# Newton steps of six attention groups as one block-diagonal product, and an ordering estimate with other prices

## The chip, the cores and the metric

The kernel runs on one core of one Trainium2 chip. The metric is the device time of one execution in microseconds (us). Engines are named as the profile names them: PE is TensorE (matmul), PEld its weight loads, DVE VectorE, ACT ScalarE, POOL GpSimd, SP the queue that issues most transfers. Each engine runs its own instructions in the order in which the program wrote them.

## The reference

A Nystrom attention over 4 batches of 8 heads (576 tokens, head size 64, 32 landmarks) is followed by two feed-forward layers over the 2304 tokens. The 32x32 matrix of the landmarks is inverted by six Newton steps.

```python
A = sm(q, k_lm)
Bm = sm(q_lm, k_lm)
C = sm(q_lm, k)
Z = Bm.transpose(0, 1, 3, 2) / (norm1(Bm) * norminf(Bm) + 1e-06)
for _ in range(6):
    Z = 2 * Z - Z @ Bm @ Z
attn = A @ Z @ C @ v
...
h = x @ w_in            # layer 1: 2304 x 512 @ 512 x 2048
g = h * tanh(softplus(h))
x = g @ w_out
...
h = x @ w_in            # layer 2, with silu
g = h * (1.0 / (1.0 + np.exp(-h)))
out = g @ w_out
```

## The kernel before, in words

**Attention groups.** The 32 heads are worked in eight groups of four heads (`Group`, g = 0 to 7, two per batch), each head on 32 of the 128 partitions. A group makes transposes of k and q (tiles `Tk`, `Tq`), the landmark means (`lmT`), the scores (`Tk,lmT` and `Tq,lmT`), the softmax of C (`ec`, transposed to `ect` and multiplied with `vn`), the softmax of A (`at`, kept as `a_t`) and the matrix Bm (`eb`, `bn`). `newton` then runs the six steps. Its state `yu` has two parts per head: 32 columns that hold the iterated product and 64 columns that hold the right side, which is carried through the steps. A step is: PE makes `y` times `yu` of each head, DVE forms twice `yu` less the product. `each` writes the product of a step as four matmuls of 32x32 weights, one per head, each on its own 32 rows and 32 columns of the PE array (tiled matmuls below). At the end one matmul of `yu` with `bd`, the block-diagonal form of Bm scaled by `rc`, gives `ut`. `main` makes `bd` once, ahead of the Newton steps.

**Layers.** Layer 1 takes `ut` times the decoded weights (`wa`, the projection, tiled matmuls of 512 columns) to `wp`, then per unit six matmuls of 288 columns to `h` (`h<-at,wp`), Mish on ACT to `z`, a split of `z` in two halves `g` (ACT and POOL), and twelve matmuls of 288 columns to `y` (`y<-g,wo`). There are 128 units, 64 of them from the first half of the inner dimension, and the units of a batch need that batch's two groups done. Layer 2 (`h<-xg,wf`, `y<-wo,xg` and others) follows. The weights arrive as 64-bit words and are decoded by ACT, DVE and POOL (`wst` to `m`, `wa`, `wo`).

**What sets the order.** Nothing is ordered by hand. `Line` holds an estimate of when each engine will be free and when each tile will be written: every operation goes through `issue` (L196 to L226 in the profile), which adds `cost` to the estimated time and then writes the instruction. Chains (a group's `main`, `c_side`, `a_side`, a decode, a projection) are generators that are stepped when the estimate says that their input is ready (`step`, `run`), and the units of layer 1 are written between them. So a changed price changes where in each engine's order every later instruction stands, and which of two engines gets an operation that either can do. Where the estimate sees PE with too little work, before all groups are done, the main loop writes pairs of transposes of `ident` that nobody reads, in the PE order; they are called fillers below. Almost every instruction has line L226, since `issue` writes it.

**Tables of ACT.** Exp (for `eb`, `ec`, `at`), Mish and Silu come from tables that ACT has to load when it goes from one to another (`ACT_TABLE_LOAD`). The estimate before has no price for it.

Of the kernel before, what the change touches and what calls it, by code (L numbers as in the profile page):

```python
# [11 lines left out]
FP32 = mybir.dt.float32  # L12
# [47 lines left out]
def width(ap):  # L60
    return ap.size() // ap.shape[0]


class Line:
# [7 lines left out]
    WINDOW, ENOUGH = 4.096 / 1.2, 3060  # L72
    AGAIN = {"V": 0.12, "A": 0.12, "P": 0.1, "T": 0.0}
    FIXED = {"V": 0.07, "A": 0.1, "P": 0.05, "T": 0.0133}
    EACH = {"V": 1.04e-3, "A": 0.82e-3, "P": 2.29e-3, "T": 0.417e-3}

    def __init__(self, nc):
        self.nc = {"V": nc.vector, "A": nc.scalar, "P": nc.gpsimd, "T": nc.tensor}
        self.free = dict.fromkeys(["V", "A", "P", "T", "D", "W"], 0.0)
        self.now = 0.0  # L80
        self.free["D"] = 0.45
        self.end = 0.0
        self.last = set()
        self.past = collections.deque()
        self.held = {"V": collections.deque(), "P": collections.deque()}
        self.busy, self.seen = {}, {}
        self.chains = []
        self.small = False
        self.count = itertools.count()

    def cost(self, e, name, kw):
        src = kw.get("in_", kw.get("in0"))
        n = width(src if name == "tensor_reduce" else kw["out"])
        psum = src is not None and src.space == bass.MemoryType.PSUM
        more = 0.0
        if e == "T":
            tiled = kw["out"].shape[0] < 96 and "lhsT" in kw
            if tiled and (kw["out"].start_partition() or kw["lhsT"].start_partition()):
                return 0.027 * self.clock()
            n *= self.clock() * self.columns(kw)  # L100
        elif e == "A":
            more = -0.04 if psum else 0.0
            more += 0.14 if "accum_out" in kw else 0.09 if kw.get("func") == ACTF.Ln else 0.0
        elif e == "P" and name == "tensor_scalar":
            n *= 0.46
        elif e == "V" and name in ("copy", "tensor_copy", "tensor_scalar", "scaled"):
            if not psum:
                n *= 0.5
            elif n < 300:
                n += 50  # L110
            more = 0.06 if hasattr(kw.get("scalar1"), "space") else 0.0
        elif e == "V" and name == "reciprocal" and n > 1:
            more = 0.09
        elif e == "V" and name == "tensor_reduce" and n > 1000:
            more = 0.9
        return self.FIXED[e] + more + n * self.EACH[e]

    @staticmethod
    def span(ap):
# [71 lines left out]
    def issue(self, engines, name, kw, bias=0.0):  # L191
        def start(e):
            at = max(self.now, self.free[e], self.depend(e, name, kw))
            return self.alone(e, at, name, kw)

        e = min(engines, key=lambda e: start(e) + self.cost(e, name, kw) + (bias if e == "V" else 0.0))  # L196
        at = start(e)
        if e == "T":
            small = kw["out"].shape[0] < 96
            if self.small and not small:  # L200
                at = max(at, self.free["T"] + 0.055)
            self.small = small
        end = at + self.cost(e, name, kw)
        if e == "T":
            tick = int(at / self.WINDOW)
            rows = kw["lhsT" if "lhsT" in kw else "in_"].shape[0]
            part = rows * kw["out"].shape[0] / 16384 * self.columns(kw)
            self.past.append((at, width(kw["out"]) * part))
            self.busy[tick] = self.busy.get(tick, 0) + width(kw["out"]) * part
        if self.holds(e, name, kw):  # L210
            self.held[e].append((at, end))
            while len(self.held[e]) > 24:
                self.held[e].popleft()
        self.free[e] = end
        self.end = max(self.end, end)
        self.last.add(e)
        self.record(e, kw, end)
        if name == "copy" and e != "A":
            name = "tensor_copy"
        if name == "scaled":  # L220
            k = dict(out=kw["out"], in_=kw["in_"])
            if e == "A":
                name, kw = "activation", dict(k, func=ACTF.Copy, scale=kw["scalar1"])
            else:
                name, kw = "tensor_scalar", dict(out=kw["out"], in0=kw["in_"], scalar1=kw["scalar1"], scalar2=None, op0=ALU.mult)
        r = getattr(self.nc[e], name)(**kw)  # L226
        return r

    def transfer(self, engine, **kw):
        ap = kw["out"] if kw["out"].space == bass.MemoryType.SB else kw["in_"]  # L230
        start = max(self.now, self.free["D"], self.depend("D", "dma", kw))
        self.free["D"] = start + width(ap) * ap.shape[0] * 4 / 0.36e6
        end = self.free["D"] + 2.1
        self.end = max(self.end, end)
        self.last.add("D")
        self.record("D", kw, end)
        return engine.dma_start(**kw)  # L237
# [110 lines left out]
def kernel(  # L348
# [99 lines left out]
    def until(cond):  # L448
        while not cond():
            yield "W"  # L450
# [549 lines left out]
    class Group:  # L1000
# [98 lines left out]
        def main(self):  # L1099
# [37 lines left out]
            for h in range(HG):  # L1137
# [56 lines left out]
            Ring.give(py)  # L1194
            yield "V"

            bd = self.bd = s_p.tile([128, HG, LM], FP32, tag="bd", name="bd")
            V.scalar_tensor_tensor(
                out=bd,
                in0=bn.rearrange("p (o l) -> p o l", o=1).to_broadcast([128, HG, LM]),  # L1200
                scalar=rc,
                in1=mask,
                op0=ALU.mult,
                op1=ALU.mult,
            )
            marks.add((g, "y"))
            yield "T"
            yield from until(marked((g, "u")))
# [3 lines left out]
        def each(out, lhsT, rhs, **kw):  # L1212

            for h in range(HG):
                r = slice(32 * h, 32 * h + 32)
                T.matmul(out=out[r], lhsT=lhsT[r], rhs=rhs[r], start=True, stop=True)

        def newton(self):

            yu, g = self.yu, self.g  # L1220
            for it in range(6):
                lo = 0 if it < 5 else LM
                yield from until(self.banks.ready)
                pn = self.banks.take([128, LM + D], FP32)
                self.each(pn[0][:, lo:], yu[:, 0:LM], yu[:, lo:])
                yield "V"
                yn = s_p.tile([128, LM + D], FP32, tag="yu", name="yu", bufs=4)
                V.scalar_tensor_tensor(
                    out=yn[:, lo:], in0=yu[:, lo:], scalar=2.0, in1=pn[0][:, lo:], op0=ALU.mult, op1=ALU.subtract
                )  # L1230
                Ring.give(pn)
                yu = yn
                yield "T"
            yield from until(self.banks.ready)
            pu = self.banks.take([128, HG * LM], FP32)
            r = slice(64 * self.hg, 64 * self.hg + 64)
            T.matmul(
                out=pu[0][r], lhsT=yu[:, LM:], rhs=self.bd.rearrange("p h l -> p (h l)"), start=True, stop=True
            )
            yield "W"  # L1240
            VA.copy(out=ut_t[self.b][r].rearrange("p h l -> p (h l)"), in_=pu[0][r])
# [290 lines left out]
```

## Time and profile before

| what | value |
|---|---|
| time, median of 3 runs | 858.45 us (857.98 to 859.84) |
| span of the profiled execution, first to last instruction | 855.9 us |
| median less span, what lies around it | 2.55 us |
| PE busy | 824.3 us (96%) |
| DVE busy | 515.6 us (60%) |
| ACT busy | 450.6 us (53%) |
| POOL busy | 288.1 us (34%) |

The page gives the span of one execution. Attention lies in its first 223 us (beside layer 1 from about 50 us on), layer 1 ends at about 467 us, layer 2 at 849 us. An engine's busy time is the union of its instructions; on PE an instruction's row reaches past the start of the next one, so for PE the distance from start to start is what an instruction costs in a stream.

### The profile page before, as it was taken

How to read it: one execution, taken by the hardware profiler on the slowest of the kernel's cores; microseconds unless marked ns; L12 is line 12 of the kernel's file. 1: busy time of each engine (PE TensorE's matmuls, PEld its weight loads, DVE VectorE, ACT ScalarE, POOL GpSimd, SP SyncE). 2: the span in 40 equal slices, each digit the busy share in tenths (PEclk: the TensorE clock that was granted, in tenths of full speed). 3: DMA queues.
4: the chain of work that ended last, by engine and by line, in shares of the span. 5: the costliest groups of instructions: out<-in, count | busy, mean ns of one | idle time of the engine just before them, and what ended most of it. 6: DMA issues, size and time to landing. Idle time of an engine off the chain costs nothing.

```text
span 855.9 us, 15972 instructions
## 1 busy us (share of the span) xinstructions
PE 824.3 (96%) x6084; PEld 726.1 (85%) x6084; DVE 515.6 (60%) x1030; ACT 450.6 (53%) x997; POOL 288.1 (34%) x331
## 2 busy tenths in 40 slices
PE   7999989899999999999999999999999999999996
PEld 5877767676899989989999898898898898998885
DVE  4976644453586958414516999767555567555542
ACT  5574776667555565433425755544544454544432
POOL 4241524342355555624323434311223221232210
PEclk9999999999999999999999999999999999999999
DMA  9874225200345554241125422101400000200002
GB/s 246 237 224 154 59 55 139 57 29 2 106 148 176 157 197 155 80 129 56 57 79 156 152 99 87 37 1 38 111 1 1 0 1 8 67 1 2 0 1 75
DMA packets 42254, 72.36 MB, mean 85 GB/s; under 512 B 5056, under 2 KB 31680, under 8 KB 42176
## 3 DMA queue, kind: packets, MB, share of 16 engines
q1 hardware_dynamic: 41600, 70.54, 27.1%
q8 instruction: 48, 0.79, 0.4%
q10 hardware_dynamic: 576, 0.79, 0.3%
q14 instruction: 30, 0.25, 0.1%
HBM read 57.15 MB, written 14.16 MB: 83 GB/s over the span
## 4 chain that ended last, share of the span: by engine, by line
PE 86%; ACT 7%; DMA 3%; issue 1%; DVE 1%; SPq 1%; POOL 0%; ACTq 0%; POOLq 0%; DVEq 0%
PE y L226 47%; PE h L226 31%; PE t L226 8%; ACT L226 3%; ACT z L226 1%; DMA wst<-in_moe_w_in_dram 1%; SPq L237 1%; DMA kn<-in_k_dram 1%; ACT g L226 1%; ACT ec L226 1%; DMA wst<-in_moe_w_out_dram 1%; DMA wst<-ys 0%; ACT at L226 0%; DMA out_dram<-ysb 0%; ACT wp L226 0%
## 5 line engine op out<-in xcount | busy, mean ns | idle before, releaser
L226 PE MATMUL y<-g,wo 128*128 128x288 f32 x1536 | 235.0, 301 | 1.4 <-POOL g L226 1.4
L226 PEld LDWEIGHTS y<-g,wo 128*128 128x128 f32 x1536 | 209.8, 188 | 15.3 <-issue 9.8
L226 PE MATMUL y<-wo,xg 128*128 128x512 f32 x693 | 179.8, 394 | 0.0
L226 POOL TENSOR_TENSOR g<-z,g 128x288 fp32r<-128x288 f32 x128 | 114.5, 905 | 174.3 <-ACT g L226 150.5
L226 PEld LDWEIGHTS y<-wo,xg 128*128 128x128 f32 x693 | 128.4, 188 | 20.9
L226 DVE TENSOR_TENSOR z<-h,z 128x384 f32<-128x384 f32 x164 | 89.4, 554 | 70.9 <-PE h L226 68.8
L226 PE MATMUL h<-at,wp 128*128 128x288 f32 x768 | 121.0, 302 | 5.8 <-ACT z L226 5.7
L226 PEld LDWEIGHTS h<-at,wp 128*128 128x128 f32 x768 | 106.3, 188 | 19.1 <-ACT z L226 8.8
L226 ACT ACTIVATE z<-h 128x288 f32<-128x288 f32 x128 | 51.6, 413 | 73.9 <-PE h L226 71.5
L226 ACT ACTIVATE z<-z 128x384 f32<-128x384 f32 x94 | 49.2, 525 | 34.3 <-DVE z L226 34.0
L226 POOL TENSOR_TENSOR wo<-m,wo 128x512 fp32r<-128x512 f32 x32 | 46.5, 1454 | 54.7 <-ACT wo L226 47.7
L226 DVE SCALAR_TENSOR_TENSOR m<-wst,m 128x512 int32<-128x512 int32 x64 | 61.9, 968 | 1.1
L226 PE MATMUL h<-xg,wp 128*128 128x384 f32 x288 | 58.0, 336 | 1.5 <-DVE z L226 1.5
L226 PE MATMUL h<-xg,wf 128*128 128x384 f32 x288 | 57.9, 336 | 0.4 <-DVE z L226 0.4
L226 ACT CAST g<-z 128x288 fp32r<-128x288 f32 x123 | 51.8, 435 | 7.4 <-PE y L226 6.2
L226 PEld LDWEIGHTS h<-xg,wp 128*128 128x128 f32 x288 | 51.3, 188 | 5.0 <-DVE z L226 1.9
L226 PEld LDWEIGHTS h<-xg,wf 128*128 128x128 f32 x288 | 51.2, 188 | 3.9 <-DVE z L226 0.9
L226 DVE TENSOR_TENSOR xg<-z,xg 128x384 fp32r<-128x384 f32 x73 | 41.4, 570 | 20.9 <-ACT xg L226 20.6
L226 POOL TENSOR_TENSOR wf<-m,wf 128x256 fp32r<-128x256 f32 x20 | 16.2, 809 | 96.8 <-ACT wf L226 96.8
L226 PE MATMUL y<-wo,wp 128*128 128x512 f32 x171 | 44.9, 394 | 0.0
L226 ACT ACT_TABLE_LOAD x31 | 39.8, 1283 | 1.7 <-PEq L1516 0.7
L226 DVE TENSOR_TENSOR wp<-t,wp 128x512 fp32r<-128x512 f32 x32 | 20.6, 685 | 30.5 <-ACT wp L226 30.4
(229 smaller groups left out, 1179.8 us busy)
## 6 DMA issues: line engine op xcount, KB each, us to landing
wst<-in_moe_w_out_dram SPq DMA_DIRECT2D x32, 512.0 KB, 5.8
wst<-in_moe_w_in_dram SPq DMA_DIRECT2D x28, 512.0 KB, 5.4
kn<-in_k_dram SPq DMA_DIRECT2D x32, 144.0 KB, 5.3
vn<-in_v_dram SPq DMA_DIRECT2D x8, 576.0 KB, 6.1
yh<-ysb SPq DMA_DIRECT2D x32, 144.0 KB, 1.9
ysb<-yh SPq DMA_DIRECT2D x32, 144.0 KB, 2.9
ys<-ysb SPq DMA_DIRECT2D x32, 144.0 KB, 2.0
qn<-in_q_dram SPq DMA_DIRECT2D x28, 144.0 KB, 3.6
```

Source lines behind the costliest of these rows:

```text
L226: r = getattr(self.nc[e], name)(**kw)
L237: return engine.dma_start(**kw)
```

## The change

Two things are changed. For groups 2 to 7 a Newton step is one matmul of the whole array: `blocks` writes the current `y` of the four heads as a block-diagonal 128x128 matrix `bd` (one DVE operation with a mask), and one matmul with `bd` as weights takes the place of the four tiled ones. Groups 0 and 1 keep the tiled form. The block-diagonal form of Bm is now made after the last step, in the same tile. And the estimate in `Line` has other prices: ACT pays for a change of table, a tiled matmul has a price that depends on how many run at once, with a price for going to the tiled form and for going back, and rates of POOL, ACT, the fp32 transposes and the transfers are different.

```diff
-    EACH = {"V": 1.04e-3, "A": 0.82e-3, "P": 2.29e-3, "T": 0.417e-3}
+    EACH = {"V": 1.04e-3, "A": 0.82e-3, "P": 2.67e-3, "T": 0.417e-3}
+    TABLES = {ACTF.Exp: "exp", ACTF.Mish: "mish", ACTF.Silu: "silu"}
+    LOAD = 1.3
+    TO_TILES, FROM_TILES, WEIGHTS = 0.092, 0.273, 0.107
...
-            tiled = kw["out"].shape[0] < 96 and "lhsT" in kw
-            if tiled and (kw["out"].start_partition() or kw["lhsT"].start_partition()):
-                return 0.027 * self.clock()
+            if "lhsT" not in kw:
+                return 0.002 + n * 2 * self.clock() * self.EACH["T"]
+            if kw["out"].shape[0] < 96:
+                at_once = 128 // kw["out"].shape[0] * (2 if kw["lhsT"].shape[0] == 64 else 1)
+                if kw["lhsT"].shape[0] == 128:
+                    at_once = 1
+                first = 0.0 if self.small else max(0.0, self.WEIGHTS - n * 2 * self.EACH["T"])
+                return first + n * 4 * self.clock() * self.EACH["T"] / at_once
...
+            if self.table_of(name, kw) not in (None, self.table):
+                more += self.LOAD
...
-                at = max(at, self.free["T"] + 0.055)
+                at = max(at, self.free["T"] + self.FROM_TILES)
+            elif small and not self.small:
+                at = max(at, self.free["T"] + self.TO_TILES)
...
-        self.free["D"] = start + width(ap) * ap.shape[0] * 4 / 0.36e6
+        rate = 0.24e6 if ap.shape[0] < 64 else 0.3e6 if ap.shape[0] < 128 else 0.4e6
+        self.free["D"] = start + width(ap) * ap.shape[0] * 4 / rate
...
+        def blocks(self, y, by):
+
+            V.scalar_tensor_tensor(
+                out=self.bd,
+                in0=y.rearrange("p (o l) -> p o l", o=1).to_broadcast([128, HG, LM]),
+                scalar=by,
+                in1=mask,
+                op0=ALU.mult,
+                op1=ALU.mult,
+            )
...
             yu, g = self.yu, self.g
+            bd = self.bd.rearrange("p h l -> p (h l)")
+            whole = g > 1
             for it in range(6):
                 lo = 0 if it < 5 else LM
+                if whole:
+                    yield "V"
+                    self.blocks(yu[:, 0:LM], 1.0)
+                    yield "T"
                 yield from until(self.banks.ready)
                 pn = self.banks.take([128, LM + D], FP32)
-                self.each(pn[0][:, lo:], yu[:, 0:LM], yu[:, lo:])
+                if whole:
+                    T.matmul(out=pn[0][:, lo:], lhsT=bd, rhs=yu[:, lo:], start=True, stop=True)
+                else:
+                    self.each(pn[0][:, lo:], yu[:, 0:LM], yu[:, lo:])
...
+            yield "V"
+            self.blocks(self.bn, self.rc)
+            yield "T"
```

In the rows below, the counts are those of the program: a tiled or an fp32 matmul against weights is one row here and two instructions in the trace; a filler is one of both. All instructions of `issue` stand at L226 before and at L256 after.

PE, the last Newton steps of group 3, before. `yu` of 32x96 and 32x64 are Newton steps, `h<-at` and `y<-g,wo` units of layer 1, `lmT` the landmark scores of group 4:

```order
L226 MATMUL y<-g,wo 128x288 x6
L226 MATMUL t<-yu 32x96 x4
L226 MATMUL h<-at_637,wp 128x288 x2
L226 MATMUL t<-lmT 32x32 x4
L226 MATMUL h<-at_637,wp 128x288 x2
L226 MATMUL t<-yu 32x96 x4
L226 MATMUL h<-at_637,wp 128x288 x6
L226 MATMUL t<-yu 32x64 x4
```

The same steps of group 3 after:

```order
L256 MATMUL t<-yu,bd 128x96
L256 MATMUL y<-g,wo 128x288 x17
L256 MATMUL t<-yu,bd 128x96
L256 MATMUL y<-g,wo 128x288
L256 MATMUL t<-yu,bd 128x64
L256 MATMUL y<-g,wo 128x288 x13
L256 MATMUL t<-bd,yu 64x128
```

Each row of four tiled matmuls is one whole matmul now; between the last three steps stand 17 and 1 matmuls of layer 1, where 4 (with four small tiled ones) and 6 stood.

PE, the first two Newton steps of group 3, before (`ident,kn` and `ident,qn` are transposes of group 4):

```order
L226 MATMUL h<-at_637,wp 128x288 x2
L226 MATMUL t<-yu 32x96 x4
L226 MATMUL h<-at_637,wp 128x288 x2
L226 MATMUL t<-ident,kn 128x128 x3
L226 MATMUL h<-at_637,wp 128x288 x2
L226 MATMUL t<-yu 32x96 x4
L226 MATMUL y<-g,wo 128x288 x2
```

The second and the third step of group 3 after (`h<-ident` are fillers, `Tk,lmT` the scores of group 4):

```order
L256 MATMUL h<-ident 128x128 x4
L256 MATMUL t<-yu,bd 128x96
L256 MATMUL h<-ident 128x128 x2
L256 MATMUL t<-lmT 32x32 x4
L256 MATMUL h<-ident 128x128 x16
L256 MATMUL t<-Tk,lmT 32x288 x8
L256 MATMUL h<-ident 128x128 x2
L256 MATMUL y<-g,wo 128x288 x12
L256 MATMUL h<-at_671,wp 128x288 x6
L256 MATMUL h<-ident 128x128 x16
L256 MATMUL y<-g,wo 128x288 x2
L256 MATMUL t<-yu,bd 128x96
```

Where the order before has only matmuls of layer 1 between the steps, 40 fillers stand now.

PE, from the scores of group 5 to the next matmul that needs a bank of the ring `t`, before:

```order
L226 MATMUL t<-Tk,lmT 32x288 x8
L226 MATMUL h<-at_1334,wp 128x288 x4
L226 MATMUL y<-g,wo 128x288 x20
L226 MATMUL t<-Tq,lmT 32x288 x8
L226 MATMUL y<-g,wo 128x288 x4
```

The same place after:

```order
L256 MATMUL t<-Tk,lmT 32x288 x8
L256 MATMUL h<-at_1359,wp 128x288 x2
L256 MATMUL y<-g,wo 128x288 x24
L256 MATMUL h<-at_1359,wp 128x288 x10
L256 MATMUL t<-bt 32x32 x4
```

36 matmuls of layer 1 stand between the scores and the next user of a bank, where 24 stood.

Counted over the whole PE order: the Newton steps of groups 2 to 7 are 36 in both; the places where PE goes from other work to tiled matmuls fall from 94 to 61; the fillers rise from 208 to 292, all 84 of the difference ahead of layer 1's second half; the matmuls of the layers are the same in number. DVE has 36 more operations `bd<-yu,mask`, and ACT 29 table loads in place of 31.

## Rows read from the trace of the kernel before

**Rows 1.** The page: engine totals, and the chain that ended last, by engine.
```profile
PE 824.3 (96%) x6084; PEld 726.1 (85%) x6084; DVE 515.6 (60%) x1030; ACT 450.6 (53%) x997; POOL 288.1 (34%) x331
PE 86%; ACT 7%; DMA 3%; issue 1%; DVE 1%; SPq 1%; POOL 0%; ACTq 0%; POOLq 0%; DVEq 0%
```
**Rows 2.** Busy time by stretch: length; PE, PEld, DVE, ACT, POOL; clock, DMA share, GB/s.
```profile
0.00:47.00 47.00, 42.13 (x534) 33.73 (x534) 36.01 (x98) 24.61 (x62) 16.31 (x29) 1.00 0.90 242
47.00:83.20 36.20, 34.63 (x384) 26.56 (x384) 24.99 (x67) 23.75 (x50) 11.36 (x10) 1.00 0.59 193
83.20:223.40 140.20, 129.83 (x1447) 98.92 (x1448) 65.92 (x200) 97.44 (x200) 52.09 (x61) 1.00 0.21 57
...
sum 855.90, PE 824.32 PEld 726.11 DVE 515.64 ACT 450.64 POOL 288.11; mean PE 137.39 PEld 121.02 DVE 85.94 ACT 75.11 POOL 48.02
```
**Rows 3.** What PE waited for, us in total, times, longest.
```profile
PE t L226 <- ACT ec L226: 6.6, 6, 1.5
PE h L226 <- ACT z L226: 5.7, 8, 1.0
```
**Rows 4.** PE in order of time around two Newton steps: start, us, operation, count.
```profile
101.44 0.42 PE L226 MATMUL h<-at,wp 128*128 128x288 f32 x2
101.79 0.37 PE L226 MATMUL t<-yu 32*32 32x96 f32 x8
102.09 0.54 PE L226 MATMUL h<-at,wp 128*128 128x288 f32 x2
102.46 0.49 PE L226 MATMUL t<-ident,kn 128*128 128x128 f32 x3
102.71 0.51 PE L226 MATMUL h<-at,wp 128*128 128x288 f32 x2
103.15 0.37 PE L226 MATMUL t<-yu 32*32 32x96 f32 x8
103.45 0.54 PE L226 MATMUL y<-g,wo 128*128 128x288 f32 x2
```
**Rows 5.** PE in order of time: rates of whole matmuls, fillers, and of `bd,yu`.
```profile
42.22 2.17 PE L226 MATMUL t<-Tk,twice 128*128 128x128 f32 x18
...
48.01 1.75 PE L226 MATMUL y<-ident 128*128 128x128 f32 x14
...
83.54 0.43 PE L226 MATMUL t<-bd,yu 128*64 128x128 f32 x2
83.90 0.40 PE L226 MATMUL h<-at,wp 128*128 128x288 f32 x1
...
450.48 8.16 PE L226 MATMUL y<-g,wo 128*128 128x288 f32 x60
```
**Rows 6.** PE, then ACT, in order of time around the longest `ec` wait.
```profile
109.96 1.64 PE L226 MATMUL t<-Tk,lmT 64*32 64x288 f32 x16
111.53 2.89 PE L226 MATMUL y<-g,wo 128*128 128x288 f32 x20
115.93 0.43 PE L226 MATMUL t<-bd,yu 128*64 128x128 f32 x2 [1.51 <-ACT ec L226]
...
113.99 1.28 ACT L226 ACT_TABLE_LOAD   x1
115.28 0.50 ACT L226 ACTIVATE ec<-t,nmc 128x288 f32<-128x288 f32 x1
```
**Rows 7.** Groups of DVE and ACT over the whole span: busy us, mean ns, idle before.
```profile
L226 DVE SCALAR_TENSOR_TENSOR yu<-yu,t 128x96 f32<-128x96 f32 x35 | 8.8, 251 | 29.5 <-PE t L226 27.1 <-issue 2.3
L226 DVE SCALAR_TENSOR_TENSOR bd<-bn,rc,mask 128x128 f32<-128x128 f32 x8 | 4.6, 569 | 0.0
...
L226 ACT ACT_TABLE_LOAD x31 | 39.8, 1283 | 1.7 <-PEq L1516 0.7 <-PE h L226 0.4
```
**Rows 8.** PE in order of time: two Newton steps of group 7, one after the other.
```profile
212.44 0.37 PE L226 MATMUL t<-yu 32*32 32x96 f32 x8
...
213.47 0.37 PE L226 MATMUL t<-yu 32*32 32x96 f32 x8
```

More of the change, by code (lines that the diff above doesn't have):

```diff
@@ L88, in __init__ @@
         self.small = False
+        self.table = "exp"
         self.count = itertools.count()
@@ L96, in cost @@
         if e == "T":
[L97 to L99 removed]
+            if "lhsT" not in kw:
[6 more added lines that the diff above has]
+                return first + n * 4 * self.clock() * self.EACH["T"] / at_once
+            if n == 512:
+                more = 0.005
+            if self.columns(kw) == 4:
+                n = max(n, 64)
             n *= self.clock() * self.columns(kw)
@@ L102, in cost @@
             more = -0.04 if psum else 0.0
-            more += 0.14 if "accum_out" in kw else 0.09 if kw.get("func") == ACTF.Ln else 0.0
+            more += 0.1 if "accum_out" in kw else 0.0
+            if name == "scaled":
+                more += 0.1
+            if src is not None and not psum and abs(src.ap[-1][0]) == 2:
+                more += 0.045
+            if self.table_of(name, kw) not in (None, self.table):
+                more += self.LOAD
         elif e == "P" and name == "tensor_scalar":
             n *= 0.46
+        elif e == "P" and "in1" in kw and not kw["in1"].ap[-1][0]:
+            n *= 0.73
         elif e == "V" and name in ("copy", "tensor_copy", "tensor_scalar", "scaled"):
@@ L116, in cost, with table_of @@
         return self.FIXED[e] + more + n * self.EACH[e]
+    def table_of(self, name, kw):
+        return self.TABLES.get(kw.get("func")) if name == "activation" else None
     @staticmethod
@@ L198, in issue @@
         if e == "T":
-            small = kw["out"].shape[0] < 96
+            small = kw["out"].shape[0] < 96 and "lhsT" in kw
             if self.small and not small:
-                at = max(at, self.free["T"] + 0.055)
+                at = max(at, self.free["T"] + self.FROM_TILES)
+            elif small and not self.small:
+                at = max(at, self.free["T"] + self.TO_TILES)
+        end = at + self.cost(e, name, kw)
+        if e == "T":
             self.small = small
-        end = at + self.cost(e, name, kw)
+        elif e == "A":
+            self.table = self.table_of(name, kw) or self.table
         if e == "T":
@@ L1195, in main @@
             yield "V"
[L1197 to L1205, printed above, removed]
+            self.bd = s_p.tile([128, HG, LM], FP32, tag="bd", name="bd")
             marks.add((g, "y"))
@@ L1237, in newton @@
             T.matmul(
-                out=pu[0][r], lhsT=yu[:, LM:], rhs=self.bd.rearrange("p h l -> p (h l)"), start=True, stop=True
+                out=pu[0][r], lhsT=yu[:, LM:], rhs=bd, start=True, stop=True
             )
```

## The prediction

> **What bounds the kernel now.** I read the page's totals first: PE is busy 96% of the span and holds 86% of the chain that ended last; DVE, ACT and POOL have much free time [rows 1]. PE runs its instructions in order, so the span can be written as an account of PE alone: work of the layers and of attention, fillers, and waits. Whatever the change does to another engine counts only where it alters one of these three. The account by stretch [rows 2] shows where there are waits: 4.9 us of PE's first 47 us (47.00 less 42.13), 1.6 us up to 83.2, 10.4 us from there to the end of attention (140.20 less 129.83), and the rest of the 31.6 us (855.90 less 824.32) in the layers behind it and at the end, where the matmuls are the same in number before and after. The granted clock is 1.00, so 2.4 GHz, in each of these stretches, so the clock has no part in the sum. What PE waited for is ACT in nearly all cases: 6.6 us in 6 waits for `ec`, 5.7 us in 8 waits for `z` [rows 3].
>
> The cause of the longest of these waits can be read off. After the scores PE has 20 matmuls of layer 1 (111.53), and is then to write a bank which `ec` still reads. ACT had to load the table of Exp first, from 113.99 to 115.27; PE stood 1.51 us [rows 6]. There are 31 such loads of 1283 ns [rows 7], 39.8 us of ACT time for which the estimate that makes the order has no price.
>
> **The change part by part.**
>
> *Whole Newton steps.* What a visit to the tiled form costs PE is read from two visits: from 101.44 to 103.45 are 2.01 us [rows 4]. In them lie six matmuls of 288 columns, at 8.16/60 = 0.136 us, and three transposes at the rate of whole fp32 passes, 2.17/18 = 0.12 us [rows 5]: 0.82 + 0.36 = 1.18. The remaining 0.83 us are two visits, 0.42 us each, though the four matmuls themselves stand for 0.30 us (101.79 to 102.09); the rest is the way into the tiled form and out. Visits fall from 94 to 61, so 33 x 0.42 = 13.9 us go; three steps shared a visit with another tiled product and give only their own 0.30 each, 0.9 us. What takes their place is 36 whole matmuls. The trace has none with 96 columns. The nearest rows are the whole fp32 passes `Tk,twice`, two of which take 0.24 us, and `bd,yu`, which takes 0.36 us from start to the next start (83.54 to 83.90) and has half of the array's columns [rows 5]. I take 0.24, since the shape of the weights is the same, and keep 0.36 for the range: 8.6 or 13.0 us. The term is -13.9 - 0.9 + 8.6 = **-6.2 us**, with -1.8 as its other end. That counts in full only where PE is the limit; before 83 us it may turn into fillers or waits, and this is part of the account below.
>
> *Fillers.* 84 more of them, each 1.75/14 = 0.125 us [rows 5]: **+10.5 us**. PE can't skip them. They stand where the new estimate sees PE with nothing to do: most of them between the first projection and the third Newton step of group 3, that is roughly between 47 and 105 us of the trace before. Whether they cost anything depends on what they displace: if PE had to wait there, the filler takes the place of a wait and the two cancel.
>
> *Waits.* So the waits decide. In the third stretch nearly all are for ACT, behind table loads. The order shows what the new price does there: between the scores of group 5 and the next user of a bank stand 36 matmuls for 24, so 4.9 us for 3.3 us at 0.136. I went through the same place in the other groups: it grows for groups 4, 6 and 7 too (20 matmuls to 18 fillers and 20 matmuls, 18 to 26, 20 to 24), and shrinks for group 3 (30 to 24, though ACT has the Exp table at hand there by its order). The wait in rows 6 needed 4.2 us of PE time, 20 matmuls and 1.51; 4.9 covers that and 3.3 does not. I take the 10.4 us of the third stretch down to 3.5: not to nothing, since some gaps stay short (the last two whole steps of group 3 have one matmul between them) and since no price is exact. In the second stretch 1.6 us go to 0.6, in the first 4.9 to 4.1 by eight more fillers: **-8.7 us** together. The ends are 0, and -12.8 if nothing is left in the second and third stretch.
>
> *DVE.* 36 new operations `bd<-yu,mask`. The same operation takes 569 ns on average in the trace, stretched in some cases [rows 7], so some 20 us, on an engine that is busy 65.92 of 140.20 us where most of them run [rows 2]. Its free time covers it. But each lies in the chain of a Newton step: PE, DVE (`yu`, 251 ns), DVE (`bd`), PE. Two steps of group 7 stood 1.03 us apart with four matmuls of layer 1 between them [rows 8]; with the new operation a step needs some 1.3 to 1.6 us. Six steps make a group 2 to 3.5 us later. This costs nothing as long as PE has units of layer 1 to run, and the order says that it has: with the last group's `bd,yu` 666 matmuls of the units are done instead of 588.
>
> *Rates of POOL and the transfers, choices of engine.* They move work between DVE, ACT and POOL (g on DVE 14 times for 5, `lmq` sums of groups 0 and 1 on DVE), and three loads on SP. I cost this at nothing, since PE covers it in the layers, with 1.5 us to either side for the first 47 us, where PE waits on the others.
>
> *The sum.* -6.2 + 10.5 - 8.7 = -4.4 us against the span of 855.9, so 851.5. What lies around the span, 2.55 us, I leave as it is: 854.0 against the median of 858.45.
>
> **Rivals.**
>
> *All waits go* (12%). With 12.8 us in place of 8.7: -6.2 + 10.5 - 12.8 gives -8.5 us, 850.0. For it: each long wait has the same cause, and this cause is now priced. Against: group 3 and its short gaps.
>
> *Nothing moves* (19%). The waits fall by only half of what I take, 4.3 us, and the rest is taken by waits elsewhere: 858.5. For it: PE's work rises by 4.3 us (10.5 less 6.2) whatever else happens, and so half of the gain has to be there to break even.
>
> *The slack is gone: slower* (20%). The order before also had PE too fast: a Newton step was priced 4 x 0.027 + 0.055 = 0.16 us where it takes 0.42 [rows 4]. Over 94 visits that is some 24 us which the other engines had beyond the estimate, and that paid for a good part of the 39.8 us of loads. Now both are priced, and each PE instruction stands close behind its input; where DVE's `bd` comes 0.3 us later than estimated (569 ns against the 251 of `yu`), PE stands at the whole matmul. With the waits as long as before the time is 858.45 - 6.2 + 10.5 = 862.8. It decides if on the mean PE waits 0.24 us at each of the 36 steps (8.7/36). Against it: by the order, all but three of the thirty gaps between whole steps hold more than 1.3 us of PE work.
>
> *ACT pays more for a load than its row* (3%). If ACT were held behind each load for as long again, the new price would be short by more than a microsecond at each of 29 loads, and the waits of the third stretch would stay: -6.2 + 10.5 - 1.8 = +2.5, 861.0. In the trace it isn't held: the load that begins at 113.99 takes 1.28 us, and `ec` begins at 115.28 [rows 6]. The Trainium skill, "ScalarE: Activation LUTs", section "What ACT_TABLE_LOAD costs", gives about 1283 ns for the load and about 1380 ns of drain on top of it for every switch. The trace agrees with the first figure and shows nothing of the second; by the page the price of 1.3 would be half of what it ought to be.
>
> **How the numbers follow.** My forecast (46%) has 851 to 856.7. A measurement of this kernel tells about 0.2%, 1.7 us, from no change. Faster are the forecast and the first rival, 58%; within 0.2% is the second, 19%; slower are the last two, 23%. For the range I take 849.0, a little below the first rival's time, to 862.0, which leaves out about half of the slow cases and what lies lower.
>
> **What would show it.** PE's busy time should stay within 5 us of 824 (+10.5, -6.2), with 33 fewer visits, and the whole matmul should show 0.24 us from start to start where its input was ready. The waits of PE for `ec` should fall from 6.6 us to under 3, and PE's idle time in attention from 16.8 us to about 8. DVE's busy time should rise by 15 to 25 us. If a new wait for `bd` or `yu` on DVE of over 4 us is in PE's list, the third rival is right; if PE's idle time falls as I say and the time does not, the fillers or the whole step cost more than I took.

## The result, and the profile after

The changed kernel takes 846.86 us (median of 4 runs, 846.40 to 849.57) against 858.42 for the kernel before on the same chip: a ratio of 0.9873, 95% interval 0.9856 to 0.9889. The direction was forecast, the size was not: 846.86 lies 7.1 us below the 854.0 and below the range. The experiments will show that about as much separates two orders of the same kernel that differ by nothing of meaning. Of all executions behind the medians here, one, of a nudged kernel, ran at a granted clock of 0.56 and took 1316.34 us; it is left out.

The page of the kernel after, totals and chain, which answer to [rows 1]:

```profile
span 844.5 us, 15708 instructions
PE 824.5 (98%) x5952; PEld 736.4 (87%) x5952; DVE 531.1 (63%) x1100; ACT 442.3 (52%) x969; POOL 271.2 (32%) x317
PE 88%; ACT 4%; DVE 3%; DMA 3%; issue 1%; SPq 1%; POOL 0%; ACTq 0%; DVEq 0%; POOLq 0%
```

PE's busy time is what it was (824.5 for 824.3); its idle time fell from 31.6 to 20.0 us. So the gain, by this account, lies wholly in idle time, although PE has 84 more fillers to run. By stretch (length; PE busy; clock, DMA share, GB/s), for the stretches of [rows 2] and two behind them:

```profile
0.00:47.00 47.00, 42.99 (x522) 0.96 0.81 216
47.00:83.20 36.20, 36.02 (x383) 1.00 0.62 187
83.20:223.40 140.20, 136.57 (x1388) 1.00 0.23 67
223.40:464.00 240.60, 237.55 (x1831) 1.00 0.42 135
464.00:620.00 156.00, 153.35 (x761) 1.00 0.21 65
```

Length less busy time gives 4.0, 0.2, 3.6, 3.1 and 2.7 us of idle time. Before it was 4.9, 1.6 and 10.4 in the first three; in the last two it was 4.1 and 3.6, as these rows of the kernel before show, which stand here for the first time:

```profile
223.40:464.00 240.60, 236.51 (x1828) 1.00 0.39 126
464.00:620.00 156.00, 152.44 (x769) 1.00 0.25 79
```

In the first stretch the granted clock of this execution was 0.96, not 1.00. The fall lies between 20 and 30 us (first row: the kernel after). The second row is of the kernel without late fillers, the second experiment below; it has the same order up to the first projection and shows no fall:

```profile
20.00:30.00 10.00, 8.80 (x135) 0.83 0.82 189
20.00:30.00 10.00, 8.69 (x167) 1.00 0.96 209
```

Their first projections start at 44.46 and 43.10 us:

```profile
44.46 1.72 PE L256 MATMUL t<-Tk,twice 128*128 128x128 f32 x13
43.10 2.16 PE L259 MATMUL t<-Tk,twice 128*128 128x128 f32 x17
```

So the clock, which the prediction gave no part, had one of about a microsecond here, and one execution of an order can differ from the next by as much.

What PE waited for after, which answers to [rows 3] (us in total, times, longest): the 6.6 us for `ec` are 0.8, and the new operation `bd` holds PE for 0.6.

```profile
PE h L256 <- ACT z L256: 3.9, 5, 1.2
PE h L256 <- DVE z L256: 2.5, 2, 1.5
...
PE t L256 <- ACT ec L256: 0.8, 2, 0.5
PE t L256 <- DVE bd L256: 0.6, 2, 0.4
```

A whole step in the order of time on PE (start, us, operation, count), to be held against [rows 4]:

```profile
162.63 1.44 PE L256 MATMUL y<-g,wo 128*128 128x288 f32 x9
163.91 0.36 PE L256 MATMUL t<-yu,bd 128*128 128x96 f32 x2
164.05 0.51 PE L256 MATMUL y<-g,wo 128*128 128x288 f32 x2
...
165.15 0.93 PE L256 MATMUL y<-g,wo 128*128 128x288 f32 x5
165.91 0.36 PE L256 MATMUL t<-yu,bd 128*128 128x96 f32 x2
```

The next matmul starts 0.14 us after the step's two passes begin, and the five matmuls ahead of the second one take 0.08 us more than 5 x 0.136: a whole step costs 0.22 us, where a tiled visit cost 0.42. On DVE and ACT (busy us, mean ns, idle before), answering to [rows 7]:

```profile
L256 DVE SCALAR_TENSOR_TENSOR bd<-yu,mask 128x128 f32<-128x128 f32 x36 | 11.6, 326 | 0.2
...
L256 ACT ACT_TABLE_LOAD x29 | 37.2, 1283 | 6.1 <-PE h L256 4.9 <-PEq L1562 0.7
```

The new operation takes 326 ns, not 569. (It multiplies by the number 1.0, where the one that was taken for its price reads its scalar from the tile `rc`.) ACT still makes 29 loads of 1283 ns.

### The profile page after: what moved, and what is told of

The parts are those of the page before. It is cut to its first block, busy times and chain, and to the rows that moved or that the text cites. A ratio compares the mean times of both kernels' runs of the same rounds, so it can differ in the third digit from the quotient of the medians.

```text
span 844.5 us, 15708 instructions
## 1 busy us (share of the span) xinstructions
PE 824.5 (98%) x5952; PEld 736.4 (87%) x5952; DVE 531.1 (63%) x1100; ACT 442.3 (52%) x969; POOL 271.2 (32%) x317
## 4 chain that ended last, share of the span: by engine, by line
PE 88%; ACT 4%; DVE 3%; DMA 3%; issue 1%; SPq 1%; POOL 0%; ACTq 0%; DVEq 0%; POOLq 0%
PE y L256 48%; PE h L256 32%; PE t L256 8%; DMA wst<-in_moe_w_in_dram 1%; ACT L256 1%; DMA out_dram<-ysb 1%; DVE m L256 1%; ACT z L256 1%; SPq L268 1%; DMA kn<-in_k_dram 1%; DVE z L256 0%; DMA wst<-ys 0%; DVE wa L256 0%; ACT ysb L256 0%; DVE yu L256 0%
## 5 line engine op out<-in xcount | busy, mean ns | idle before, releaser
L256 PE MATMUL y<-g,wo 128*128 128x288 f32 x1536 | 228.9, 299 | 0.6 <-POOL g L256 0.5
L256 PEld LDWEIGHTS y<-g,wo 128*128 128x128 f32 x1536 | 209.0, 188 | 11.4 <-issue 9.9
L256 PE MATMUL y<-wo,xg 128*128 128x512 f32 x693 | 179.8, 394 | 0.0
L256 POOL TENSOR_TENSOR g<-z,g 128x288 fp32r<-128x288 f32 x127 | 110.3, 880 | 165.3 <-ACT g L256 113.6
L256 PEld LDWEIGHTS y<-wo,xg 128*128 128x128 f32 x693 | 128.4, 188 | 21.0
L256 DVE TENSOR_TENSOR z<-h,z 128x384 f32<-128x384 f32 x161 | 87.9, 555 | 71.5 <-PE h L256 68.5
L256 PE MATMUL h<-at,wp 128*128 128x288 f32 x768 | 122.2, 301 | 2.8 <-ACT z L256 2.7
L256 PEld LDWEIGHTS h<-at,wp 128*128 128x128 f32 x768 | 106.7, 188 | 13.0 <-issue 7.4
L256 ACT ACTIVATE z<-h 128x288 f32<-128x288 f32 x128 | 51.6, 415 | 75.8 <-PE h L256 73.0
L256 ACT ACTIVATE z<-z 128x384 f32<-128x384 f32 x93 | 48.9, 526 | 40.1 <-DVE z L256 39.4
L256 POOL TENSOR_TENSOR wo<-m,wo 128x512 fp32r<-128x512 f32 x32 | 45.5, 1427 | 61.3 <-ACT wo L256 58.5
L256 PE MATMUL h<-xg,wp 128*128 128x384 f32 x288 | 58.1, 336 | 1.6 <-DVE z L256 1.5
L256 PE MATMUL h<-xg,wf 128*128 128x384 f32 x288 | 57.5, 335 | 0.0
L256 DVE TENSOR_TENSOR xg<-z,xg 128x384 fp32r<-128x384 f32 x74 | 43.0, 581 | 21.6 <-ACT xg L256 21.4
L256 PEld LDWEIGHTS h<-xg,wp 128*128 128x128 f32 x288 | 51.2, 188 | 5.5 <-DVE z L256 2.4
L256 ACT CAST g<-z 128x288 fp32r<-128x288 f32 x114 | 47.7, 437 | 12.4 <-PE y L256 11.2
L256 PEld LDWEIGHTS h<-xg,wf 128*128 128x128 f32 x288 | 51.3, 188 | 3.1
L256 DVE SCALAR_TENSOR_TENSOR m<-wst,m 128x512 int32<-128x512 int32 x64 | 53.0, 836 | 0.7
L256 PE MATMUL y<-wo,wp 128*128 128x512 f32 x171 | 44.9, 394 | 0.0
L256 ACT ACT_TABLE_LOAD x29 | 37.2, 1283 | 6.1 <-PE h L256 4.9
L256 POOL TENSOR_TENSOR wf<-m,wf 128x256 fp32r<-128x256 f32 x17 | 12.6, 743 | 82.6 <-ACT wf L256 82.6
L256 ACT CAST xg<-z 128x384 fp32r<-128x384 f32 x74 | 38.0, 513 | 1.6
```

## Experiments in the order of the kernel after

Three kernels keep the changed kernel's order of instructions and alter only what is issued. Nothing else moves in them, so they price a part by itself, to within the microsecond by which executions of one order differ.

**Whole or tiled, in one order.** Each whole product is emitted as the four tiled ones that it replaces; the estimate still believes in one.

```
-    T.matmul(out=pn[0][:, lo:], lhsT=bd, rhs=yu[:, lo:], ...)
+    for h in range(HG):
+        r = slice(32 * h, 32 * h + 32)
+        nc.tensor.matmul(out=pn[0][r, lo:], lhsT=yu[r, 0:LM], rhs=yu[r, lo:], ...)
```

> The order of the changed kernel on every engine, but each whole Newton step is written as four tiled matmuls at the same place (the block-diagonal operation on DVE is kept, unused by these steps). It measures the price of a step in place: 95 visits in place of 61. With 0.42 us for a visit and 0.22 for a whole step: +7 us, 854. With 0.55 for a visit: +11 to +12, 858. If the waits take it up: under +3.

Measured: 853.52 us (0.9941, 0.9921 to 0.9960), 6.7 above the kernel after. PE's busy time:

```profile
PE 830.4 (98%) x6168; PEld 733.2 (86%) x6168; DVE 528.4 (62%) x1100; ACT 442.5 (52%) x969; POOL 272.9 (32%) x317
```

It is 5.9 us more. The Newton term of the sum, -6.2, is right. (Each of the two profiles has one short fall of the clock ahead of the end of attention, the kernel after at 20 to 30 us, this one in 100 to 120, where it averages 0.91. So the difference of the two profiles holds to about a microsecond.)

**No late fillers.** The 150 fillers behind the start of the first projection are planned but not issued, so PE waits where they stood. (They compute nothing that is used.)

```
+    line.mute = ("P", 0, 0) in marks
     for i in range(2):
         T.transpose(out=b_[0][:, i * 128:i * 128 + 128], in_=ident, identity=ident)
+    line.mute = False
```

> The order of the changed kernel on every engine, without the 150 fillers that stand behind the first projection (142 of 292 are left). It measures what fillers cost in place. Theory (they stand where PE would wait): PE's busy time falls by 10 to 18 us, its waits rise by nearly as much, and the time is within 2 us of 846.9, unless the granted clock falls. Rival (they hold up work that is ready): 835 to 842.

Measured: 847.95 us (0.9882, 0.9864 to 0.9899); the span is 844.5, that of the kernel after to the tenth. The totals of its page, and its second and third stretch (length; PE busy; clock):

```profile
PE 812.7 (96%) x5802; PEld 723.2 (86%) x5802; DVE 531.1 (63%) x1100; ACT 442.1 (52%) x969; POOL 272.7 (32%) x317
```

```profile
47.00:83.20 36.20, 29.07 (x300) 0.93 0.69 218
83.20:223.40 140.20, 132.17 (x1313) 0.97 0.21 57
```

Busy time falls by 11.8 us, 0.079 for each filler, and idle time rises by as much. The 0.079 is a net figure. The rows of the instructions on `ident` alone (the kernel after, then this one) fall by 22.8 us, or 0.15 for each filler, so the rows of other instructions got longer by 11.0 without the fillers:

```profile
0.00:844.50 844.50, 76.61 (x496) 1.00 0.28 86
0.00:844.50 844.50, 53.77 (x346) 0.99 0.28 86
```

A part of that is the granted clock. It is 1.00 in the kernel after and falls to 0.93 and 0.97 in the second and third stretch here, so some of the work ran at the lower of the two levels, 1.2 GHz. One such place, here and then in the kernel after, from a Newton step to the next unit:

```profile
114.63 0.46 PE L259 MATMUL t<-yu,bd 128*128 128x96 f32 x2 [3.09 <-ACT ec L259]
...
119.15 1.16 PE L259 MATMUL h<-at,wp 128*128 128x288 f32 x6
```
```profile
116.35 0.46 PE L256 MATMUL t<-yu,bd 128*128 128x96 f32 x2 [0.47 <-ACT ec L256]
...
119.45 1.06 PE L256 MATMUL h<-at,wp 128*128 128x288 f32 x6
```

Without fillers PE had waited 3.09 us; the clock from 114.6 to 119.2 was then 0.65, and the same instructions took 4.52 us for 3.10. This kernel's lead over the kernel after, 1.72 us at the first of these rows, is 0.30 at the second. It had begun with 1.36 us, since in this execution the first projection starts at 43.10 for 44.46. That the two spans agree to the tenth is therefore partly luck. The medians differ by 1.1 us, within the spread of either kernel's runs. What can be said is that the late fillers cost no measurable time: for the most part they stand in place of waits. If they gain anything, it is about a microsecond, by the clock, and that is not shown.

**The link on DVE doubled.** `bd<-yu,mask` is issued twice in each of the 36 steps.

```
+    if y is not self.bn:
+        nc.vector.scalar_tensor_tensor(out=self.bd, in0=y..., scalar=by, in1=mask, ...)
```

> The changed kernel with the block-diagonal operation of each whole step written twice on DVE, the second one unknown to the estimate: 36 more operations of 0.33 us, each in the chain of a step. Theory (PE has other work between steps): under +2 us. Rival (PE stands at the whole matmul for what DVE is late): +6 to +12 us, waits of PE for bd over 5 us.

Measured: 852.81 us (0.9938, 0.9923 to 0.9952), 5.95 above the kernel after, for 36 x 0.33 = 11.9 us of added chain. PE's waits show where (L1252 is the second `bd`):

```profile
PE t L256 <- DVE wp L256: 1.7, 3, 0.9
PE t L256 <- DVE bd L1252: 1.6, 4, 0.7
...
PE t L256 <- DVE bd L256: 1.2, 2, 0.8
```

More of it counts than the theory allowed. The link isn't covered by layer 1 throughout: an order is laid out for the price that it knows, and of what went beyond that price here a half came through.

## Experiments with other orders

Everything else goes through the estimate and so gives another order. I split the change in its two halves first.

**Whole steps with the old estimate; tiled steps with the new one.** The first is the changed kernel with the class `Line` of before, the second the kernel before with the new `Line`.

```
whole, old estimate:  class Line of before + class Group of after
tiled, new estimate:  class Line of after  + class Group of before
```

> The whole Newton steps of the changed kernel, ordered by the estimate of the kernel before; 252 fillers, 60 visits to the tiled form. Theory (the Newton term was mis-sized: a visit costs 0.5 to 0.6 us, and the waits fall because of the prices): 34 visits fewer give 10 us, 44 fillers more cost 5.5, and the waits stay near the 31.6 us of before: 854 us, idle time of PE in the third stretch near 10. Rival (the whole steps alone bring it, the prices nothing): 847 to 849, idle time near that of the changed kernel.

> The tiled Newton steps of the kernel before, ordered by the new estimate; 266 fillers, 97 visits. Theory: 58 fillers more cost 7 us, 3 visits more 1.5, and the waits fall by 10 to 11 us: 856 to 857. Rival (the prices bring it all): 847 to 849. Rival (the whole steps bring it all): 858 or more.

Measured: 866.37 us (1.0089, 1.0065 to 1.0113) and 854.91 (0.9959, 0.9943 to 0.9975). Alone the whole steps lose 8, the estimate wins 3, together they win 11.6. I took this for a coupling of the two, as the rival of the missing slack has it. That did not hold, as the nudges below show.

**Without the price of a load, without the new prices of PE, without the new rates.** Each takes one part of the new estimate back, with whole steps.

```
-    LOAD = 1.3
+    LOAD = 0.0
```
```
-    TO_TILES, FROM_TILES, WEIGHTS = 0.092, 0.273, 0.107
+    TO_TILES, FROM_TILES, WEIGHTS = 0.0, 0.273, 0.107
...
-                at = max(at, self.free["T"] + self.FROM_TILES)
+                at = max(at, self.free["T"] + 0.055)
...                                                     # and PE's cost as before
```
```
-    EACH = {..., "P": 2.67e-3, ...}
+    EACH = {..., "P": 2.29e-3, ...}
...
-        rate = 0.24e6 if ap.shape[0] < 64 else 0.3e6 if ap.shape[0] < 128 else 0.4e6
+        rate = 0.36e6
...                                                     # and no factor 0.73 for POOL
```

> The changed kernel with the price of a table load at 0, the other new prices kept; 310 fillers, 61 visits. Theory: the waits for ec and z come back in the third stretch, 5 us or more, and 18 more fillers cost 2: 852 to 855. Rival (the waits fell through the other prices): within 1.5 us of 846.9, waits for ec under 2 us.

> The changed kernel with the PE prices of before (a tiled matmul 0.027, 0.055 for the way back, fillers at the old price), the load price and the other new prices kept; 314 fillers, 63 visits. Theory after the first four runs (prices work together: a PE that is estimated too fast puts instructions ahead of their input): slower than the changed kernel by 4 to 10 us, with more fillers and more waits. Rival (only the load price counts): within 2 us of 846.9.

> The changed kernel with POOL's and the transfers' rates of before, all else kept; 280 fillers, 60 visits. Theory: within 3 us of 846.9, since neither stands in PE's list of waits for more than 1.4 us. Rival (the rates bring a good part): 850 to 856.

Measured: 865.76 us (1.0083, 1.0060 to 1.0106), 853.18 (0.9948, 0.9931 to 0.9965) and 850.09 (0.9907, 0.9892 to 0.9922). Without the load's price all of the gain is gone. PE's idle time is 31.7 us, as it was before the change, and the third stretch (length; PE busy; clock) has 11.3 us of idle time again, about as many as before the change:

```profile
83.20:223.40 140.20, 128.94 (x1290) 0.99 0.21 57
```

**The price of a load alone.** The converse: the estimate of before with that price and nothing else, for tiled and for whole steps.

```
+    TABLES = {ACTF.Exp: "exp", ACTF.Mish: "mish", ACTF.Silu: "silu"}
+    LOAD = 1.3
...
+            if self.table_of(name, kw) not in (None, self.table):
+                more += self.LOAD
```

> The kernel before, with nothing changed but the price of a table load (1.3 us) in its estimate; steps stay tiled, 94 visits, 234 fillers for 208. Theory (the unpriced loads are the cause of the waits in attention, and the tiled steps' unpriced 0.26 us a visit hid a part of them): PE's idle falls from 31.6 us to 22 to 26, the fillers stand in place of waits, 850 to 854. Rival (the price works only together with the prices of PE's tile changes, since without them the estimate still has PE too early by some 24 us over the visits): 855 to 859. A third reading, that every new order scatters by 5 us whatever the price: 855 to 866, with waits for ec no shorter than the 6.6 us of before.

> Whole steps with the old estimate (866.4 us) and the price of a load added, nothing else of the new estimate. Theory (what the whole steps alone lost, 8 us against before, was lost to loads for which PE no longer had time to spare): the price gives back most of it, 848 to 853, with idle of PE at 22 to 27 us for 37.4. Rival (the prices of PE's tile changes and the rates are as necessary as the load): 857 to 862, as they cost 6.3 and 3.2 us when taken out alone.

Measured: 843.55 us (0.9829, 0.9813 to 0.9845) and 841.18 (0.9803, 0.9787 to 0.9818). Both are faster than the kernel after; with whole steps it is the fastest kernel of the study. PE's totals of the latter, and its first three stretches (length; PE busy; clock):

```profile
PE 816.1 (97%) x5902; PEld 730.9 (87%) x5902; DVE 529.9 (63%) x1083; ACT 444.9 (53%) x980; POOL 288.7 (34%) x331
```

```profile
0.00:47.00 47.00, 42.09 (x529) 1.00 0.88 237
47.00:83.20 36.20, 35.12 (x378) 1.00 0.62 201
83.20:223.40 140.20, 138.25 (x1408) 1.00 0.22 59
```

In the third stretch 2.0 us of idle time are left of 10.4. So the remaining prices of the new estimate seemed to cost 5.7 to 11.4 us together, although taking back either set alone had made the kernel slower. That is what a scatter looks like, and it had to be measured.

**A nudge without meaning.** Six kernels get 5 ns more in the estimate's price of each DVE operation. On the chip that stands for nothing, but the order differs from the first rows on.

```
-    FIXED = {"V": 0.07, ...}
+    FIXED = {"V": 0.075, ...}
```

> The kernel before with 5 ns more in the estimate's price of every DVE operation (0.075 us for 0.07), a change that has no meaning on the chip and yet gives another order from the first rows on. Theory (the time belongs to the prices): 856.5 to 860, as the kernel before. Rival (an order scatters by several us whatever the price): 3 us or more off 858.4 to either side. If the unpriced loads are the cause, it stays above 852 in either case, with waits for ec of 4 us or more.

> The kernel after with the same 5 ns nudge; 324 fillers for 292. Theory: 845 to 848.5. Rival: 3 us or more off 846.9 to either side; then the losses of 3 to 6 us that showed when one price was taken back (853.2 with the old PE prices, 850.1 with the old rates) can't be told from scatter.

> Whole steps with the old estimate (866.4 us), nudged by the same 5 ns. The nudge moved the kernel before by 11.1 us, the changed one by 6.5, and the two with the load's price alone by 3.4 and 1.4. Theory now (without the price of a load the table loads fall where they will, so such orders lie anywhere between 856 and 872, and whole steps are neither better nor worse there): 856 to 872, and the 8 us by which whole steps lost to the kernel before mean nothing. Rival (whole steps cost 8 us in an order that doesn't know the loads): 874 to 880, 8 us above the nudged kernel before.

> Tiled steps with the whole new estimate (854.9 us), nudged by the same 5 ns. Theory now (with the price of a load in it an order lies between 841 and 856 and the new estimate's other prices win nothing here): 845 to 857. Rival (the other prices cost something by themselves, 11 us with tiled steps): 853 to 857 once more, above both kernels that have the load's price alone (843.6 and 846.9).

> Tiled steps, old estimate plus the price of a load (843.6 us), with the 5 ns nudge. Theory: 842 to 845. Rival: 3 us or more off. If it stays below 852 the load's price is worth more than the scatter even so.

> Whole steps, old estimate plus the price of a load (841.2 us), with the 5 ns nudge. Theory: 839.5 to 843. Rival: 3 us or more off. If it is within 1.7 us of 843.6 or above it, the whole steps' 2.4 us under this estimate are not shown by that pair alone.

Measured, in us (the last column is the mean of the two; the ratios of the nudged ones, down the rows: 1.0121, 1.0098 to 1.0144; 1.0089, 1.0064 to 1.0113; 0.9858, 0.9836 to 0.9880; 0.9810, 0.9783 to 0.9837; 0.9917, 0.9890 to 0.9943; 0.9932, 0.9909 to 0.9955):

| estimate | steps | as it is | nudged | mean |
|---|---|---|---|---|
| old | tiled (before) | 858.4 | 869.5 | 864.0 |
| old | whole | 866.4 | 866.7 | 866.5 |
| old + load | tiled | 843.6 | 846.9 | 845.2 |
| old + load | whole | 841.2 | 842.5 | 841.9 |
| new | tiled | 854.9 | 851.4 | 853.2 |
| new | whole (after) | 846.9 | 853.4 | 850.1 |

A nudge moves a kernel by 0.3 to 11.1 us. The kernel before, nudged (span, PE's totals, then its waits):

```profile
span 868.7 us, 15956 instructions
PE 829.0 (95%) x6074; PEld 729.1 (84%) x6074; DVE 520.2 (60%) x1030; ACT 447.5 (52%) x989; POOL 295.3 (34%) x337
```

```profile
PE h L226 <- ACT z L226: 5.9, 10, 1.1
PE t L226 <- ACT ec L226: 5.1, 5, 1.9
PE h L226 <- DVE z L226: 4.2, 4, 1.7
PE t L226 <- ACT Tk L226: 3.7, 3, 2.1
```

Its span is 12.8 us longer in these profiles. Idle time makes 8.1 of them (39.7 for 31.6), and PE's busy time the other 4.7, with ten fillers fewer. The third stretch points to a reason for the latter: its idle time, 10.7 us, is about what it was, but its granted clock is 0.98 for 1.00:

```profile
83.20:223.40 140.20, 129.47 (x1451) 0.98 0.19 52
```

Of the five orders without the price of a load, the kernel before is the fastest, and the only one whose profile has a granted clock of 1.00 from 47 to 620 us; the other four have 0.99, and the eleven orders with the price that have a profile at full clock all have 1.00. So a part of what the waits cost seems to come through the clock; how much, no run separates.

What follows from the table:
- **The price of a load is what the change gains**: 18.8 us with tiled steps (864.0 to 845.2) and 24.6 with whole ones, each from the means of two orders. No order without it, of five (with the 865.8 above), is below 858; none with it, of twelve, is above 855. This stands clear of the scatter; the sizes hold to a few us.
- **Whole steps** take 3 us off where the load is priced (3.3 and 3.1), and 2.5 are added where it isn't. By themselves these differences don't stand above the scatter; that a step costs PE less is shown by the kernel in the same order.
- **The rest of the new estimate costs about 8 us** (845.2 to 853.2, 841.9 to 850.1). Three of the four orders with it are slower than all four that have only the load's price, the fourth (846.86) is level with the slowest of these (846.90). So a cost is likely, but which of the prices brings it is open: 853.2 and 850.1 with one set taken back lie among the orders of the full estimate.
- From 864.0 to 850.1 are -13.9: -18.8 for the load, -3.3 for the whole steps, +8.2 for the rest.

**Two attempts to go on from the kernel after.** One prices the link `bd<-yu,mask` at 0.33 us, the other takes whole steps in groups 0 and 1 too.

```
+    elif e == "V" and ... (out is 128 x 4 x 32, with in1):
+        more = 0.13
```
```
-    whole = g > 1
+    whole = True
```

> The kernel after, with the operation bd<-yu,mask priced at its measured 0.33 us, where its estimate has 0.20. 340 fillers for 292. Theory (half of that link's length shows in the time, as when it was doubled: 5.95 us for 11.9): the order leaves room for 36 x 0.13 = 4.7 us of chain, of which half was being waited for, so 844 to 846.5 with no waits for bd or yu. Rival (the link's 0.6 us of waits are all there is to win, and the other order is as good or worse): 846.5 to 852.

> The kernel after with groups 0 and 1 taking whole steps too: 52 visits for 61, 12 more whole products, 346 fillers for 292. Theory (0.42 us a visit against 0.22 a whole product where PE is the limit): 9 x 0.42 - 12 x 0.22 = 1.1 us less work, and no new wait since the fillers stand in place of waits: 844.5 to 847. Rival (in the first 47 us nothing else is there for PE, so the chain of a step sets the time, and DVE's 0.33 us is added to each of 6 steps of two groups that run side by side): 6 x 0.33 = 2 us more to 4 us more, 848 to 851.

Measured: 851.08 us (0.9917, 0.9902 to 0.9932) and 851.57 (0.9922, 0.9907 to 0.9937). Both are in the range of the orders of the new estimate, 846.9 to 854.9, so neither shows a gain or a loss of its edit in attention. One thing can be seen in the second, in PE's order of time: the first projection, which in the kernel after starts at 44.46, starts at 49.62, later as the rival had it, and by more.

```profile
49.62 2.27 PE L256 MATMUL t<-Tk,twice 128*128 128x128 f32 x18
```

## Why the prediction was wrong, by its steps

**The Newton steps, -6.2: right.** 5.9 us of busy time and 6.7 us of time in the same order. The step at 0.22 us is close to the 0.24 that I took from `Tk,twice`; the 0.36 of `bd,yu` was the wrong neighbour.

**The fillers, +10.5: the step that failed.** I wrote that a filler in place of a wait cancels with it, and then put all 84 into the sum as work, beside a forecast of waits that was already made with them. In the kernel without the late ones, all 150 together are worth nothing that can be measured: 0.0 us of the span, 1.1 us of the median, and that in their favour. Net of what other instructions lose without them, they weigh 0.079 us each in PE's busy time, not 0.125: 6.6 us for 84, so 3.9 us too much. With -6.2 the busy time should rise by 0.4; it rose by 0.1. I don't take that for proof, since the busy time too differs by 4.7 us between the kernel before and its nudged form, and the clock has a part in both figures. That the late fillers cost no measurable time in place is shown; that the fillers alone explain the 4.2 us by which the busy time was missed is not.

A filler can also be held itself: in the kernel after one stood before a bank that ACT still read.

```profile
104.27 0.74 PE L256 MATMUL h<-ident 128*128 128x128 f32 x4 [1.22 <-ACT z L256]
```

**The waits, -8.7: right in size and cause, in attention.** They fell by 9.0 us there (16.8 to 7.8), and those for `ec` from 6.6 to 0.8, under the 3 that I had named. That they stood behind unpriced table loads shows in three places. In the third stretch before, each of PE's twelve waits of over 0.3 us ended 1.7 to 2.4 us after a table load had begun on ACT. The kernel without the price has the waits again, and those with the price alone lose most of them: PE waits for `ec` 3.7 to 7.4 us in the five orders without it, and at most 2.8 in those eleven with it. The reading of the waits was too wide, though: "ACT in nearly all cases" holds in the third stretch, where the list has nothing else; over the whole span it is 14.7 of 24.2 us listed, and four of the eight waits for `z` lie behind attention, with no load before them. The two largest entries for the third stretch before (us in total, times, longest):

```profile
PE t L226 <- ACT ec L226: 5.8, 5, 1.5
PE h L226 <- ACT z L226: 3.0, 4, 1.0
```

What I left out is the 2.6 us by which PE's idle time fell behind attention (7.7 to 5.7 in the two stretches above, the rest at the end): I took it as fixed since the matmuls there are the same. But their order is drawn anew as well; the nudges say how far that can go. In the stretch from 223.4 to 464, where the kernel before has 4.1 us of idle time and the kernel after 3.1, the nudged kernel before has 6.5 us of idle time and the nudged kernel after 5.4 (length; PE busy; clock; the former first):

```profile
223.40:464.00 240.60, 234.10 (x1788) 0.99 0.38 123
```

```profile
223.40:464.00 240.60, 235.21 (x1812) 1.00 0.39 130
```

Together: PE's busy time was missed by 4.2 us (+4.3 forecast, +0.1 measured), its idle time by 2.8 (-8.7 and -11.5). That is the 7.0 us between the span forecast, 851.5, and the span measured, 844.5.

**DVE's link at nothing: not shown to be nothing.** Doubled, half of it came through. The 0.6 us of waits for `bd` say that in this order little of the single one did.

**Rates at 1.5 us to either side: not settled.** The first projection starts 2.2 us later than before in the profile (44.46 for the 42.22 of [rows 5]), but at 43.10 to 43.76 in the three kernels that have the same order up to there: the rest goes with the low clock in the head of that one execution. Nor is it a property of the rates alone: with the same ones and tiled steps it starts at 42.47, and with the old ones, whole steps and the nudge at 45.43.

**The rivals.** "All waits go" (850.0) was nearest and has the direction of the error: more waits went than I took. "Nothing moves" needed the waits to fall by 4.3 us; they fell by 9.0 in attention. "The slack is gone" looked right in the whole steps with the old estimate (866.4), but the tiled ones, nudged, take 869.5, so the slack of the tiled visits isn't needed to explain it. "ACT pays more for a load" falls: with 1.3 us as the price the waits for `ec` go. The Trainium skill, "ScalarE: Activation LUTs", section "What ACT_TABLE_LOAD costs", adds about 1380 ns of drain to the load; no run here shows it.

**What was missing altogether** is a term for the draw. The range had 849.0 as its lower end, from bounds on single terms, while two orders of the same prices lie up to 11 us apart, 6.5 for the kernel after. Nudged, it takes 853.35, as good as the forecast of 854.0. That the forecast is off by 7 us for this order and by less than one for the next says how much of any such number belongs to the order alone.

## What to carry to other kernels

Where an estimate makes the order of a kernel, each edit of a price draws a new order. Give one price a nudge that means nothing, see in several orders how far the time moves, and believe no difference of single runs that is smaller; where the same order can be kept and only the instructions exchanged, a part is priced without this scatter. Price first what an in-order engine stands behind for longest (here the table loads of ACT, whose price was worth some 20 us), and don't count as work what an idle engine is given to do.

## What the runs showed of the hardware

- 150 matmuls put where PE would otherwise wait cost no measurable time: without them 11.8 us less of busy time, the span the same, the median 1.1 us longer.
- Without them the granted clock averaged 0.93 and 0.97 in two stretches. After one wait of 3.09 us it was 0.65 for 4.6 us, and work that took 3.10 us at 1.00 took 4.52.
- A whole fp32 product of 128 x 128 weights and 96 columns costs 0.22 us among other matmuls; the four 32 x 32 products of the same step cost 0.42, of which their own time is 0.30 [rows 4].
- The DVE operation with 128 columns took 326 ns on average in 36 cases, where the eight of the same kind that I had priced it by took 569 [rows 7], and take 482 in the kernel after; these read their scalar from a tile, but whether that is why, no run here separates.
